# Chunks of x and y at different distances from the weights' buffers, modulo 512 bytes

## The chip, the cores and the metric

One NeuronCore of one Trainium2 chip runs the whole program. The metric is the device time of one launch in microseconds.

## The reference

A linear attention (8 batches, 8 heads, 576 tokens, 64 features), then two MLPs on its output of 4608 tokens by 512 features:

```python
q_s = exp(q - max(q, axis=-1));  q_s /= sum(q_s, axis=-1) + 1e-9
k_s = exp(k - max(k, axis=2));   k_s /= sum(k_s, axis=2) + 1e-9
x = q_s @ (k_s.T @ v)                                # per batch and head, then 4608 x 512
g = x @ w_gate
y = (silu(g) * (x @ w_val)) @ w_out                  # 512 -> 1536 -> 512
h = maximum(maximum(y @ w1, y @ w2), y @ w3)
out = h @ w_out2                                     # 512 -> 768 -> 512
```

q, k and v are float32, the weights are float64, the output is float32.

## The kernel before

The tokens go in 9 blocks of 512. Activations lie with their features on the partitions: x of a block is four chunks (128 features by 512 tokens each), y likewise. A float32 operand of a large product is carried as two float32r parts, hi and lo, and a product as hi*hi + hi*lo + lo*hi (`mm3`, L495). So one 128x512 chunk of a product is three TensorE instructions, each with its own load of 128 columns of weights.

A block is 60 groups in a fixed order. First MLP: for each of 12 slices of 128 hidden features a group G (x by `w_gate`), a group V (x by `w_val`) and a group O (the hidden slice by `w_out`, into four accumulators `acc`). Second MLP: for each of 6 slices W1, W2, W3 (y by a weight slice) and P (the hidden slice by the last weights). Every group is 12 TensorE instructions:

- G, V, W1 to W3 (`proj`): for each of the four chunks c the weights `whi`, `whi`, `wlo` (columns c*128 and on) are loaded, and `xhi`, `xlo`, `xhi` (or `yhi`, `ylo`, `yhi`) of chunk c are streamed, 512 columns each, into one PSUM tile `pm`.
- O (`acc_mm`): `whi`/`wlo` are loaded, `hhi`/`hlo` streamed. P: the other way round, `hhi`/`hlo` loaded and `whi`/`wlo` streamed.

While one product streams, the weights of the next are loaded. Six groups of the first block (`WHOLE`) take plain float32 operands unsplit instead (L525), in two passes each.

`split_hi` (ScalarE, L484) and `split_lo` (VectorE, L489) make `whi` and `wlo` of a group from resident float32 weights or from `plain`, which SyncE loads from a copy in DRAM. Group n's turn issues `split_lo` of n + 3, `split_hi` of n + 4, the products of n, the attention steps of the next block that stand in a table at this group, and the eviction of `pm` (`main_ev`). Both `whi` and `wlo` have five buffers. The attention of the next block makes x with `x_mm` and `x_split` (L388, L389); y is made at the end of O (L578, L579). In the first block, weights are converted from float64 on the way, for which the places of `yhi` and `ylo` serve as staging until y needs them.

The buffers are laid out in the order of their first use, so their places follow from the sizes above them. Modulo 512 bytes within a partition the ones that matter begin here, all buffers of one name alike:

```
raw_g, raw_v, raw_w1..3, kvhi, kvlo, k_sb, q_sb   128
yhi, ylo, qthi                                    224
xhi, xlo, whi, wlo, plain, s, h, hhi, hlo         352
qtlo                                              480
```

A chunk of x or y is 2048 bytes and a weight slice of 128 columns 512 bytes, so all chunks and all slices of a buffer have the same residue. By "distance" the text means the moving operand's start less that of the weights loaded meanwhile, modulo 512: 0 for x against `whi` and `wlo`, 224 - 352 = 384 for y.

Of the kernel before, what the change touches and what calls it, by code (L numbers as in the profile page):

```python
# [8 lines left out]
F32 = mybir.dt.float32  # L9
F32R = mybir.dt.float32r  # L10
# [8 lines left out]
def linear_attention_moe_moe_kernel(  # L19
# [13 lines left out]
):  # L33
    """Per block of 512 tokens: linear attention -> gated MLP -> max-of-three MLP.

    A float32 operand x of the large products is carried as hi + lo, both float32r (12
    significant bits each, so that hi + lo == x), and a product as hi*hi + hi*lo + lo*hi.
    Activations are feature-major (features on partitions) up to the last product.
    """
    nc = tc.nc  # L40
# [17 lines left out]

    ident = sb.tile([128, 128], F32, name="ident")
    raw = {  # L60
# [18 lines left out]
    }  # L79
    # For blocks of 32 by 32 to be transposed: rows are (head of a pair, half of its features,  # L80
    # token of 32), columns (pair, tokens by 32, feature of 32).
    att["qp"] = att["q"].rearrange("p r h d -> p (r h d)").rearrange("p (g n i) -> p g n i", g=HP, i=32)
    # The first block has its tokens in another order (4 p + r in row p of tile r), for long runs
    # in DRAM, and its own staging, where the second MLP's weights will be.
    w = [raw[t].rearrange("p f c n -> p (f c n)") for t in ("W1", "W2", "W3")]
    n, m = R * HH * D, HH * D

    def hrd(a, i):
# [23 lines left out]

    # ---------------------------------------------------------------- attention
    def load_k(t, b, hf):
# [67 lines left out]
    def both(a, tag):  # L182
        """a with the halves of each head's rows (of 32) exchanged."""
        o = sb.tile([128, HP, TB // 32], F32, tag=tag, name=tag)
        for i in range(4):
            p, p1 = 32 * i, 32 * (i ^ 1)
            nc.vector.tensor_copy(out=o[p:p + 32], in_=a[p1:p1 + 32])
        return o
# [163 lines left out]
    def q_t(t, c, g):  # L352
        """Blocks of 32 rows by 32 columns; they already stand where their transposes have to."""
        if g == 0:
            c["qthi"] = sb.tile([128, HP, TB], F32R, tag="qthi", name="qthi")
            c["qtlo"] = sb.tile([128, HP, TB], F32R, tag="qtlo", name="qtlo")
        hi, lo = c["qthi"][:, g, :], c["qtlo"][:, g, :]
        whole = sb.tile([128, TB], F32, tag="o", name="whole", bufs=2)
        nc.vector.transpose(out=whole, in_=t["qp"][:, g].rearrange("p n i -> p (n i)"))
        nc.scalar.copy(out=hi, in_=whole)  # L360
        nc.vector.tensor_tensor(out=lo, in0=whole, in1=hi, op=ALU.subtract)
# [19 lines left out]
    def x_split(px, j, pg):  # L381
        if pg == 0:
            st["x", j] = (
                sb.tile([128, KC, TB], F32R, tag="xhi", name="xhi"),
                sb.tile([128, KC, TB], F32R, tag="xlo", name="xlo"),
            )
        x = st["x", j]
        nc.scalar.copy(out=x[0][:, pg, :], in_=px)  # L388
        nc.vector.tensor_tensor(out=x[1][:, pg, :], in0=px, in1=x[0][:, pg, :], op=ALU.subtract)  # L389

    # ---------------------------------------------------------------- weights
    groups = []
# [26 lines left out]
    def stage_tile(i):  # L419
        """Until the first MLP's output needs their place, four more of them."""  # L420
        if i >= RING or i % 7 < 3:
            return sb.tile([128, 2 * TB], U32, tag="stage", name="stage", bufs=3)
        t, e = divmod(i % 7 - 3, 2)
        return ring[t][:, e, :]

    def load_w(n):
        """The first block takes the weights as they come: pairs of words (low, high) of float64."""
        if n >= len(groups):
            return
        j, kind, f = groups[n]  # L430
        if j == 0:
            staged[n] = stage_tile(done["load"])
            if kind in "OP":
                nc.sync.dma_start(out=staged[n], in_=src[kind][f * 128:(f + 1) * 128, :].bitcast(U32))
            else:
                nc.sync.dma_start(
                    out=staged[n].rearrange("p (c f) -> p c f", c=KC),
                    in_=src[kind][:, f * 128:(f + 1) * 128].bitcast(U32).rearrange("(c p) f -> p c f", p=128),
                )
        elif kind in "OP":  # L440
            plain[n] = sb.tile([128, TB], F32, tag="plain", name="plain", bufs=3)
            nc.sync.dma_start(out=plain[n], in_=kept[kind][f * 128:(f + 1) * 128, :])

    def convert_act(n):
        """float64 words to float32: the high word, scaled as if it were a float32, has its
        exponent field in place for a shift by 3; below float32's range it vanishes. Of the
        low word the upper three bits (0 to 7, the scale keeps it from 8) go to the high word's
        lower half, whose upper half has the sign."""
        j, kind, f = groups[n]
        if kind in "OP":  # L450
            plain[n] = sb.tile([128, TB], F32, tag="plain", name="plain", bufs=3)
        else:
            plain[n] = resident(kind, f)
        words = staged[n].rearrange("p (n t) -> p n t", t=2)
        low, high = words[:, :, 0], words[:, :, 1]
        bits = staged[n].bitcast(U16).rearrange("p (n t) -> p n t", t=4)[:, :, 2]
        nc.scalar.activation(out=plain[n], in_=high.bitcast(F32), func=AF.Abs, scale=2.0 ** -112)  # L457
        nc.scalar.activation(  # L458
            out=bits, in_=low, func=AF.Copy, scale=2.0 ** -29 * (1.0 - 2.0 ** -7), bias=-0.44
        )  # L460
# [17 lines left out]
    def split_hi(n):  # L478
# [3 lines left out]
        hi = sb.tile([128, TB], F32R, tag="whi", name="whi", bufs=5)  # L482
        lo = sb.tile([128, TB], F32R, tag="wlo", name="wlo", bufs=5)
        nc.scalar.copy(out=hi, in_=plain[n])  # L484
        parts[n] = (hi, lo)

    def split_lo(n):
        hi, lo = parts[n]
        nc.vector.tensor_tensor(out=lo, in0=plain.pop(n), in1=hi, op=ALU.subtract)  # L489

    # ---------------------------------------------------------------- main products
    def mm3(o, pairs):
# [6 lines left out]
    def proj(n, act, c0, c1):  # L499
# [3 lines left out]
        if c0 == 0:  # L503
# [3 lines left out]
        mm3(st["p", n], [  # L507
            ((whi[:, cs[c]], wlo[:, cs[c]]), (act[0][:, c, :], act[1][:, c, :]), c == 0, c == KC - 1)
            for c in range(c0, c1)
# [9 lines left out]
    def acc_mm(todo, e0, e1):  # L519
        """The products of O and P: a whole (float32) or as parts."""  # L520
        for e in range(e0, e1):
# [31 lines left out]
    def main_ev(n):  # L553
# [18 lines left out]
        elif kind == "O" and f == F1 - 1:  # L572
            y = (
                sb.tile([128, KC, TB], F32R, tag="yhi", name="yhi"),
                sb.tile([128, KC, TB], F32R, tag="ylo", name="ylo"),
            )
            for e in range(KC):
                nc.scalar.copy(out=y[0][:, e, :], in_=st["acc"][e])  # L578
                nc.vector.tensor_tensor(  # L579
                    out=y[1][:, e, :], in0=st["acc"][e], in1=y[0][:, e, :], op=ALU.subtract  # L580
                )
# [14 lines left out]

    # ---------------------------------------------------------------- schedule
    def attention(j, hf, t):
        """The steps of block j's attention for half of the heads: (slot, step)."""
        c = {}  # L600
# [31 lines left out]
    AHEAD = 3  # L632
    # The first block's conversions: LEAD groups ahead of their use, some of the second MLP earlier.
    order, quota = [], []
# [12 lines left out]
    def loads(upto):  # L647
        """Loads of the first block, in the order of the conversions."""
        while done["load"] < min(upto, GPB):
            load_w(order[done["load"]])  # L650
            done["load"] += 1
# [89 lines left out]

# When the next block's attention goes, by the group that it follows: of the first half of the
# heads and of the second, in the first block and in the others.
SLOTS_FIRST = (
# [26 lines left out]
)  # L771
# Of the first block: conversions whose staging may lie where the first MLP's output will, groups
# whose products take float32 unsplit, conversions ahead, groups that convert one more.
RING = 34
# [6 lines left out]
)  # L781
# What comes before the first group: loads, and steps for a half of the heads, a count of
# conversions or a group ("P": on GpSimd).
LOADS = (
# [45 lines left out]
```

## Time and profile before

| | |
|---|---|
| runs | 1639.6 us median of 3 (1637.58 to 1644.17) |
| profiled execution | span 1635.9 us, 18978 instructions; its own time is not given apart from the span, the median lies 3.7 us above it |
| TensorE busy | 1581.1 us, 97% (6980 products) |
| weight loads busy | 1287.1 us, 79% |
| VectorE, ScalarE busy | 939.7 us, 57%; 741.2 us, 45% |
| granted TensorE clock | 0.995 in the mean |

Busy time of TensorE is the time in which at least one product is in the array; products overlap, so their single durations (some 390 ns) add up to more. How often one starts is read from the start times in the timeline. An instruction is named out<-in; for a product the first input is the moving operand and the second the loaded weights.

### The profile page before, as it was taken

The numbers are of one execution on the slowest core, as the hardware profiler recorded it, in microseconds if no ns is written. First come the engines' busy times: TensorE is split into PE (matmuls) and PEld (weight loads), VectorE is DVE, ScalarE is ACT, GpSimd is POOL, SyncE is SP. The second block draws the span as 40 slices with busy tenths as digits, with TensorE's granted clock in tenths as the row PEclk, the third lists the DMA queues.
The fourth block names the chain that finished last, engine by engine and source line by source line (L and its number), as shares of the span: only waits on it lengthen the run. The fifth ranks groups of instructions, "written<-read, shape, count | busy, mean of one in ns | idle before, by whom it ended". The sixth has DMA issues, their size and how long they took to land.

```text
span 1635.9 us, 18978 instructions
## 1 busy us (share of the span) xinstructions
PE 1581.1 (97%) x6980; PEld 1287.1 (79%) x6980; DVE 939.7 (57%) x1589; ACT 741.2 (45%) x1234; POOL 32.4 (2%) x35
## 2 busy tenths in 40 slices
PE   2699999999999999999999999999999999999999
PEld 1487677888888888888888888888888888888887
DVE  3487785547554765467545754575546644664443
ACT  2799874343434343344334443434343433443332
POOL 1100000000000000000000000000000000000000
PEclk9899999999999999999999999999999999999999
DMA  7484654103310322120411141033102111111100
GB/s 199 119 244 155 190 154 107 33 17 72 79 48 26 68 61 65 33 54 23 111 33 43 38 105 33 16 74 74 52 26 68 52 46 39 26 42 43 33 27 32
DMA packets 197181, 112.93 MB, mean 69 GB/s; under 512 B 145888, under 2 KB 169440, under 8 KB 197088
## 3 DMA queue, kind: packets, MB, share of 16 engines
q1 hardware_dynamic: 197088, 111.72, 25.1%
q8 instruction: 55, 0.90, 0.2%
q14 instruction: 38, 0.31, 0.1%
HBM read 97.52 MB, written 14.16 MB: 68 GB/s over the span
## 4 chain that ended last, share of the span: by engine, by line
PE 89%; ACT 6%; issue 2%; DVE 1%; DMA 1%; POOL 1%; SPq 0%; DVEq 0%; POOLq 0%
PE pm L495 59%; PE acc L495 24%; PE pkv L228 3%; ACT stage L458 2%; ACT whi L484 1%; PE acc L525 1%; PE px L377 1%; PE px L376 1%; PE px L378 1%; ACT raw_w L457 0%; ACT plain L457 0%; DMA raw_w<-in_q_dram 0%; ACT ring_ylo L458 0%; ACT ring_yhi L458 0%; DMA stage<-in_moe_w_dram 0%
## 5 line engine op out<-in xcount | busy, mean ns | idle before, releaser
L495 PE MATMUL pm<-xhi,whi 128*128 128x512 f32 x864 | 339.1, 392 | 3.6 <-ACT s L558 3.6
L495 PE MATMUL pm<-xlo,whi 128*128 128x512 f32 x864 | 336.8, 390 | 0.4 <-DVE xlo L389 0.4
L495 PE MATMUL pm<-xhi,wlo 128*128 128x512 f32 x864 | 336.7, 390 | 0.0
L561 DVE TENSOR_TENSOR h<-s,pm 128x512 f32<-128x512 f32 x108 | 74.3, 688 | 334.8 <-PE pm L495 333.6
L495 PE MATMUL pm<-yhi,whi 128*128 128x512 f32 x648 | 258.3, 399 | 2.3 <-ACT s L565 1.9
L495 PE MATMUL pm<-yhi,wlo 128*128 128x512 f32 x648 | 256.0, 395 | 0.0
L495 PE MATMUL pm<-ylo,whi 128*128 128x512 f32 x648 | 255.7, 395 | 0.2 <-DVE ylo L579 0.2
L515 ACT CAST hhi<-h 128x512 fp32r<-128x512 f32 x156 | 97.5, 625 | 330.7 <-DVE h L561 211.5
L495 PEld LDWEIGHTS pm<-xhi,whi 128*128 128x128 f32 x864 | 162.5, 188 | 39.7 <-ACT s L558 5.0
L495 PEld LDWEIGHTS pm<-xlo,whi 128*128 128x128 f32 x864 | 162.6, 188 | 35.3 <-issue 1.0
L495 PEld LDWEIGHTS pm<-xhi,wlo 128*128 128x128 f32 x864 | 162.5, 188 | 33.6
L495 PE MATMUL acc<-hhi,whi 128*128 128x512 f32 x424 | 164.9, 389 | 0.0
L495 PE MATMUL acc<-hlo,whi 128*128 128x512 f32 x424 | 164.9, 389 | 0.0
L495 PE MATMUL acc<-hhi,wlo 128*128 128x512 f32 x424 | 164.9, 389 | 0.0
L495 PEld LDWEIGHTS pm<-yhi,whi 128*128 128x128 f32 x648 | 121.7, 188 | 34.1 <-ACT s L565 3.2
L558 ACT ACTIVATE s<-pm 128x512 f32<-128x512 f32 x108 | 65.4, 606 | 179.1 <-PE pm L495 179.0
L495 PEld LDWEIGHTS pm<-ylo,whi 128*128 128x128 f32 x648 | 121.7, 188 | 29.2 <-DVE ylo L579 0.5
L495 PEld LDWEIGHTS pm<-yhi,wlo 128*128 128x128 f32 x648 | 121.7, 188 | 29.1
L484 ACT CAST whi<-raw_w 128x512 fp32r<-128x512 f32 x162 | 101.1, 624 | 69.1 <-PE pm L495 55.6
L489 DVE TENSOR_TENSOR wlo<-plain,whi 128x512 fp32r<-128x512 f32 x156 | 106.8, 685 | 17.3 <-ACT whi L484 17.2
L489 DVE TENSOR_TENSOR wlo<-raw_w,whi 128x512 fp32r<-128x512 f32 x162 | 110.0, 683 | 10.2 <-ACT whi L484 10.2
L516 DVE TENSOR_TENSOR hlo<-h,hhi 128x512 fp32r<-128x512 f32 x156 | 108.0, 692 | 12.6 <-ACT hhi L515 0.7
(142 smaller groups left out, 1996.9 us busy)
## 6 DMA issues: line engine op xcount, KB each, us to landing
plain<-kept_o SPq DMA_DIRECT2D x96, 256.0 KB, 2.7
plain<-kept_p SPq DMA_DIRECT2D x48, 256.0 KB, 2.7
out_dram<-o SPq DMA_DIRECT2D x36, 256.0 KB, 2.0
stage<-in_moe_w_dram SPq DMA_DIRECT2D x17, 512.0 KB, 3.8
v_sb<-in_v_dram SPq DMA_DIRECT2D x60, 128.0 KB, 2.7
k_sb<-in_k_dram SPq DMA_DIRECT2D x56, 128.0 KB, 3.2
stage<-in_moe_w_out_dram SPq DMA_DIRECT2D x12, 512.0 KB, 3.7
stage<-in_moe_w_gate_dram SPq DMA_DIRECT2D x6, 512.0 KB, 5.0
```

The source lines that it names most:

```text
L228: nc.tensor.matmul(out=c["pkv"][:, g, :], lhsT=lhsT, rhs=rhs, start=i == 0, stop=i == R)
L376: nc.tensor.matmul(out=px[:, a:e], lhsT=hi, rhs=qhi, start=True, stop=False)
L377: nc.tensor.matmul(out=px[:, a:e], lhsT=hi, rhs=qlo, start=False, stop=False)
L378: nc.tensor.matmul(out=px[:, a:e], lhsT=lo, rhs=qhi, start=False, stop=True)
L458: nc.scalar.activation(out=bits, in_=low, func=AF.Copy, scale=2.0 ** -29 * (1.0 - 2.0 ** -7), bias=-0.44)
L484: nc.scalar.copy(out=hi, in_=plain[n])
L489: nc.vector.tensor_tensor(out=lo, in0=plain.pop(n), in1=hi, op=ALU.subtract)
L495: nc.tensor.matmul(out=o, lhsT=a, rhs=b, start=first and m == 0, stop=last and m == 2)
L515: nc.scalar.copy(out=hi, in_=h)
L516: later.append(lambda: nc.vector.tensor_tensor(out=lo, in0=h, in1=hi, op=ALU.subtract))
L558: nc.scalar.activation(out=st["s"], in_=p, func=AF.Silu)
L561: nc.vector.tensor_tensor(out=h, in0=st["s"], in1=p, op=ALU.mult)
```

## The change

Each of `xhi`, `xlo`, `yhi`, `ylo` becomes a flat tile that is 128 elements (512 bytes) longer, and its four chunks are cut from it at shifts of 0, 8, 48, 80 elements (x) and 0, 32, 48, 96 elements (y): 0, 32, 192, 320 and 0, 128, 192, 384 bytes. To make room, `wlo` has four buffers for five, taken from the pool in `split_lo` and no more in `split_hi`, and `ident` (512 bytes) lies in a part of `raw_w2` that is free until late in the first block. The names `ones` and `diag` are not used. Comments and docstrings are gone, which moves line numbers.

```diff
-    ident = sb.tile([128, 128], F32, name="ident")
...
+    spot = w[1][:, n + (R + 1) * HP * VC:]
+    ident, ones = spot[:, 0:128], spot[:, 128:256]
+    diag = spot[:, 256:512].rearrange("p (g n) -> p g n", g=HP)
...
+    XS, YS = (0, 8, 48, 80), (0, 32, 48, 96)
+
+    def chunks(tag, shifts):
+
+        t = sb.tile([128, KC * TB + 128], F32R, tag=tag, name=tag)
+        return [t[:, e * TB + d:(e + 1) * TB + d] for e, d in enumerate(shifts)]
...
-            st["x", j] = (
-                sb.tile([128, KC, TB], F32R, tag="xhi", name="xhi"),
-                sb.tile([128, KC, TB], F32R, tag="xlo", name="xlo"),
-            )
+            st["x", j] = (chunks("xhi", XS), chunks("xlo", XS))
         x = st["x", j]
-        nc.scalar.copy(out=x[0][:, pg, :], in_=px)
-        nc.vector.tensor_tensor(out=x[1][:, pg, :], in0=px, in1=x[0][:, pg, :], op=ALU.subtract)
+        nc.scalar.copy(out=x[0][pg], in_=px)
+        nc.vector.tensor_tensor(out=x[1][pg], in0=px, in1=x[0][pg], op=ALU.subtract)
...
         hi = sb.tile([128, TB], F32R, tag="whi", name="whi", bufs=5)
-        lo = sb.tile([128, TB], F32R, tag="wlo", name="wlo", bufs=5)
         nc.scalar.copy(out=hi, in_=plain[n])
-        parts[n] = (hi, lo)
+        parts[n] = (hi, None)
 
     def split_lo(n):
-        hi, lo = parts[n]
+        hi = parts[n][0]
+        lo = sb.tile([128, TB], F32R, tag="wlo", name="wlo", bufs=4)
+        parts[n] = (hi, lo)
         nc.vector.tensor_tensor(out=lo, in0=plain.pop(n), in1=hi, op=ALU.subtract)
...
-            ((whi[:, cs[c]], wlo[:, cs[c]]), (act[0][:, c, :], act[1][:, c, :]), c == 0, c == KC - 1)
+            ((whi[:, cs[c]], wlo[:, cs[c]]), (act[0][c], act[1][c]), c == 0, c == KC - 1)
...
-            y = (
-                sb.tile([128, KC, TB], F32R, tag="yhi", name="yhi"),
-                sb.tile([128, KC, TB], F32R, tag="ylo", name="ylo"),
-            )
+            y = (chunks("yhi", YS), chunks("ylo", YS))
             for e in range(KC):
-                nc.scalar.copy(out=y[0][:, e, :], in_=st["acc"][e])
+                nc.scalar.copy(out=y[0][e], in_=st["acc"][e])
                 nc.vector.tensor_tensor(
-                    out=y[1][:, e, :], in0=st["acc"][e], in1=y[0][:, e, :], op=ALU.subtract
+                    out=y[1][e], in0=st["acc"][e], in1=y[0][e], op=ALU.subtract
                 )
```

The buffers begin at the same residues as before: y at 224, x, `whi` and `wlo` at 352. So the distances are 0, 32, 192 and 320 for x's chunks 0 to 3, and 384, 0, 64 and 256 for y's: seven different values, 0 among both.

The instructions and their order on every engine stay as they were, but for the names. What changes is a wait: 186 of the subtractions into `wlo` now wait for TensorE, which has to be done with the buffer's last use. On VectorE, around the groups of the first MLP in the second block, the rows read before:

```order
L561 TENSOR_TENSOR h<-s,pm 128x512 [waits PE_49,Activation_49]
L489 TENSOR_TENSOR wlo<-raw_g,whi 128x512 [waits Activation_49]
L516 TENSOR_TENSOR hlo<-h,hhi 128x512 [waits Activation_49]
L489 TENSOR_TENSOR wlo<-raw_v,whi 128x512 [waits Activation_49]
L561 TENSOR_TENSOR h<-s,pm 128x512 [waits PE_49,Activation_49]
```

With the change, at the same place:

```order
L568 TENSOR_TENSOR h<-s,pm 128x512 [waits PE_49,Activation_49]
L496 TENSOR_TENSOR wlo<-raw_g,whi 128x512 [waits Activation_49]
L523 TENSOR_TENSOR hlo<-h,hhi 128x512 [waits Activation_49]
L496 TENSOR_TENSOR wlo<-raw_v,whi 128x512 [waits PE_49,Activation_49]
L568 TENSOR_TENSOR h<-s,pm 128x512 [waits PE_49,Activation_49]
```

One of the two subtractions into `wlo` waits for TensorE as well (PE_49); nothing has moved.

## Rows read from the trace of the kernel before

**Rows 1.** The page: span, busy time by engine, granted clock in 40 slices.

```profile
span 1635.9 us, 18978 instructions
...
PE 1581.1 (97%) x6980; PEld 1287.1 (79%) x6980; DVE 939.7 (57%) x1589; ACT 741.2 (45%) x1234; POOL 32.4 (2%) x35
...
PEclk9899999999999999999999999999999999999999
```

**Rows 2.** The page: the chain of waits that ended last, by line.

```profile
PE pm L495 59%; PE acc L495 24%; PE pkv L228 3%; ACT stage L458 2%; ACT whi L484 1%; PE acc L525 1%; PE px L377 1%; PE px L376 1%; PE px L378 1%; ACT raw_w L457 0%; ACT plain L457 0%; DMA raw_w<-in_q_dram 0%; ACT ring_ylo L458 0%; ACT ring_yhi L458 0%; DMA stage<-in_moe_w_dram 0%
```

**Rows 3.** Groups of instructions: count, busy us, mean ns of one, idle before.

```profile
L495 PE MATMUL pm<-xhi,whi 128*128 128x512 f32 x864 | 339.1, 392 | 3.6 <-ACT s L558 3.6
...
L495 PE MATMUL pm<-yhi,whi 128*128 128x512 f32 x648 | 258.3, 399 | 2.3 <-ACT s L565 1.9
L495 PE MATMUL pm<-ylo,whi 128*128 128x512 f32 x648 | 255.7, 395 | 0.2 <-DVE ylo L579 0.2
...
L495 PE MATMUL acc<-hhi,whi 128*128 128x512 f32 x424 | 164.9, 389 | 0.0
...
L495 PE MATMUL acc<-whi,hhi 128*128 128x512 f32 x200 | 78.2, 391 | 0.0
```

**Rows 4.** Timeline of PE, products with x: start us, us; twelve from first to last.

```profile
259.90 0.39 PE L495 MATMUL pm<-xhi,whi 128*128 128x512 f32 x1
...
262.62 0.39 PE L495 MATMUL pm<-xhi,whi 128*128 128x512 f32 x1
```

**Rows 5.** Timeline of PE, products with y, 24 up to `pkv`.

```profile
399.66 0.40 PE L495 MATMUL pm<-yhi,whi 128*128 128x512 f32 x1
399.90 0.39 PE L495 MATMUL pm<-ylo,whi 128*128 128x512 f32 x1
400.12 0.40 PE L495 MATMUL pm<-yhi,wlo 128*128 128x512 f32 x1
...
405.26 1.05 PE L228 MATMUL pkv<-v_sb,k_sb 128*128 128x130 f32 x8
```

**Rows 6.** Timeline of PE, a group P behind y, up to the next y.

```profile
372.84 0.40 PE L495 MATMUL acc<-whi,hhi 128*128 128x512 f32 x1
373.08 0.40 PE L495 MATMUL acc<-wlo,hhi 128*128 128x512 f32 x1
373.31 0.40 PE L495 MATMUL acc<-whi,hlo 128*128 128x512 f32 x1
373.55 0.39 PE L495 MATMUL acc<-whi,hhi 128*128 128x512 f32 x1
...
374.93 0.39 PE L495 MATMUL acc<-whi,hhi 128*128 128x512 f32 x1
...
375.61 0.40 PE L495 MATMUL pm<-yhi,whi 128*128 128x512 f32 x1
```

**Rows 7.** Timeline of PE, around `px` in two blocks.

```profile
425.60 0.40 PE L495 MATMUL acc<-whi,hlo 128*128 128x512 f32 x1
425.83 0.28 PE L376 MATMUL px<-qthi,kvhi 128*128 128x256 f32 x1
...
1422.58 0.39 PE L495 MATMUL pm<-yhi,wlo 128*128 128x512 f32 x1
1422.81 0.39 PE L376 MATMUL px<-qthi,kvhi 128*128 128x512 f32 x1
1423.05 0.40 PE L377 MATMUL px<-qtlo,kvhi 128*128 128x512 f32 x1
1423.28 0.39 PE L378 MATMUL px<-qthi,kvlo 128*128 128x512 f32 x1
1423.52 0.39 PE L495 MATMUL pm<-yhi,whi 128*128 128x512 f32 x1
```

**Rows 8.** Plain float32 products: eight passes in the timeline, and their group.

```profile
205.64 3.59 PE L525 MATMUL acc<-plain,h 128*128 128x512 f32 x8
...
L525 PE MATMUL acc<-plain,h 128*128 128x512 f32 x32 | 14.6, 598 | 0.0
```

**Rows 9.** Timeline of DVE in the second block.

```profile
302.06 0.69 DVE L489 TENSOR_TENSOR wlo<-raw_v,whi 128x512 fp32r<-128x512 f32 x1 [0.46 <-ACT whi L484]
307.09 0.69 DVE L561 TENSOR_TENSOR h<-s,pm 128x512 f32<-128x512 f32 x1 [4.34 <-PE pm L495]
```

**Rows 10.** Busy us (and instructions) of PE, PEld, DVE, ACT, POOL in a stretch of the first block.

```profile
100.00:300.00 200.00, 193.81 (x816) 150.30 (x816) 150.01 (x266) 149.21 (x212) 3.72 (x3) 0.99 0.52 155
```

More of the change, by code (lines that the diff above doesn't have):

```diff
@@ L482, in split_hi, with split_lo @@
         hi = sb.tile([128, TB], F32R, tag="whi", name="whi", bufs=5)
-        lo = sb.tile([128, TB], F32R, tag="wlo", name="wlo", bufs=5)
         nc.scalar.copy(out=hi, in_=plain[n])
+        parts[n] = (hi, None)
+    def split_lo(n):
+        hi = parts[n][0]
+        lo = sb.tile([128, TB], F32R, tag="wlo", name="wlo", bufs=4)
         parts[n] = (hi, lo)
-    def split_lo(n):
-        hi, lo = parts[n]
         nc.vector.tensor_tensor(out=lo, in0=plain.pop(n), in1=hi, op=ALU.subtract)
```

## The prediction

> **What bounds the kernel.** The page first: TensorE (PE) is busy for 97% of the span, VectorE (DVE) for 57%, ScalarE (ACT) for 45%, and the granted clock reads 9 in every slice but one, which is the 2.4 GHz level [rows 1]. The chain of waits says the same: products of `pm` at L495 make up 59% of the span and those of `acc` 24% [rows 2]. So the time is the number of TensorE instructions times their spacing, and a change pays only if it moves that spacing or makes TensorE wait.
>
> The spacing comes from the timeline, as the difference of two start times (a duration of 0.39 includes the drain, which overlaps the next product). With x as the moving operand, twelve products take 262.62 - 259.90 = 2.72 us, 226.7 ns each [rows 4]. With y, 24 products take 405.26 - 399.66 = 5.60 us, 233.3 ns each, in a pattern of a longer and a shorter one [rows 5]. Both are 128x512 with the same number type at the same clock. The groups of instructions agree: 390 to 392 ns of one with x, 395 to 399 with y, 389 with `hhi` [rows 3]. What differs is the address: x, `whi` and `wlo` begin at 352 modulo 512, y at 224. While a product streams x or y, the weights of the next product are loaded from `whi` or `wlo`, so the distance of moving operand and load is 0 for x and 384 for y. Distance does matter here, by 6.6 ns per product between these two.
>
> One more group matters. The products of P stream `whi` while `hhi` or `hlo` is loaded, at distance 0 as well, but directly behind y. There the first four begin 0.24, 0.23 and 0.24 us apart, and all twelve take 375.61 - 372.84 = 2.77 us, 230.8 ns each, although the last three are back at 0.227 [rows 6]. So 226.7 is a state that distance 0 settles into after some products; what ran before decides how soon. In O, behind x, it is there throughout (389 ns of one), in P not quite (391) [rows 3].
>
> **The change, part by part.** (1) *x leaves distance 0.* There are 3 x 864 = 2592 products with x [rows 3], 648 per chunk. Chunk 0 stays at 0; chunks 1, 2 and 3 go to 32, 192 and 320, 1944 products in all. No row has these distances. The lower bound is a product with nothing in its way: the eight passes of plain float32 products run at half rate and take 3.59 us with the 0.60 of the last [rows 8], so (3.59 - 0.60)/7 = 0.427 per pass and 213.6 at full rate. The upper bound is the other distances that the trace has at 512 columns: `px` and the y product ahead of it run at 96, 352 and 384, and those four take 1423.52 - 1422.58 = 0.94 us, 235 each, and single ones read 0.24; a product at 224 takes 425.83 - 425.60 = 0.23 us [rows 7]. Everything in the trace that is not settled lies between 230.8 and 235, on both sides of y's 233.3. I take 232 for an unknown distance, midway between P behind y and y, since those two have the most products behind them. 1944 x (232 - 226.7) = **+10.3 us**.
>
> (2) *x's chunk 0 and the O products lose their settled state.* In a G group chunk 0 follows a settled O; in a V group it follows chunk 3 of G, so half of its 648 products start unsettled: 324 x (230.8 - 226.7) = **+1.3 us**. The 3 x 424 products of O [rows 3] now stand behind x's chunk 3 as P's stand behind y; P reads 391 against O's 389, so 1272 x 2 ns = **+2.5 us**. Lower bound of both: nothing, if the new distances settle too.
>
> (3) *y.* Of 3 x 648 = 1944 products [rows 3], 486 per chunk, chunk 0 stays at 384. Chunk 1 comes to 0, three products at a time between others, so as P's unsettled ones: 486 x (230.8 - 233.3) = -1.2 us. Chunks 2 and 3 go to 64 and 256, both unknown: 972 x (232 - 233.3) = -1.3 us. Together **-2.5 us**. P stays behind y's chunk 3 as before.
>
> (4) *Four `wlo` buffers for five.* 186 subtractions on VectorE now wait for the products of the group that has just gone by. Queued behind such a subtraction are the subtraction of `hlo` and the next eviction of `pm`. A group is 2.72 us, and the `wlo` written then is used three groups, 8.2 us, later; one subtraction takes 0.69, and VectorE sits idle for 4.3 us in front of the eviction of `h` [rows 9]. So the wait is taken from idle time: 0. Without that cover, in the first block, VectorE is busy 150 of 200 us and TensorE already loses 6 [rows 10]; I allow 0 to +3 us there.
>
> (5) *`ident` in a piece of `raw_w2`, and every buffer moved by a multiple of 32 bytes:* the transposes of the first block read it before that place is converted; no term.
>
> Sum: 10.3 + 1.3 + 2.5 - 2.5 = **+11.6 us** on the profiled execution's span of 1635.9. The median of the runs, 1639.6, lies 3.7 above it, and nothing outside the span changes, so I forecast 1639.6 + 11.6 = **1651 us**, 0.7% slower.
>
> **The rule of two ports.** The row first: the same product is spaced 226.7 ns behind x and 233.3 behind y [rows 4, 5]. The Trainium skill, "SBUF — State Buffer", section "Who interferes with whom", gives TensorE two independent read ports, one for the moving operand and one for weight loads, and says that "PE and ACT never wait on anyone". By that rule no distance would matter and the sum would be 0; the two rows speak against it.
>
> The fp32 passes come within a nanosecond of one column per cycle at half rate [rows 8]. The Trainium skill, "TensorE: Matmul & The Clock Gate", section "Back-to-back issue gap", puts a lone 512-column product at N/2.4 + 2.5, an estimate of 215.8 ns; by it all five new distances could gain 11 to 18 ns a product, and the sum would be near -36 us. No fp32r row of this trace runs there.
>
> **The rivals.** With p for the mean spacing at the five unknown distances the sum is 1944(p - 226.7) + 972(p - 233.3) + 2600 ns. It is 0 at p = 228.0, and 0.5% of the time (8.2 us, about what a measurement can tell from no change) away at 225.2 and 230.8.
>
> *Free distances, faster.* If the load and the moving read pass each other unhindered at some distances, p falls below 225.2. With two of x's three new chunks and one of y's two at 213.6 and the others at 232: 1296 x -13.1 + 648 x 5.3 + 486 x -19.7 + 486 x -1.3 + 2600 ns = -21 us, **1618 us**. For it: distance matters, and most residues have no row. Against: the rows at distances 0, 96, 224, 352 and 384 show nothing steadily under 226.7 [rows 4 to 7]. Chance 0.23.
>
> *Near balance.* The new distances settle like 0 does, or mix, p between 225.2 and 230.8: 226.7 everywhere gives -6.4 us plus the 2.6 of term 2 and chunk 1, **about 1636**. Chance 0.22.
>
> *Distance does nothing*, and y is slower for another reason (what the evictions beside it do, say): **1640**. For it only the rule above. Chance 0.08.
>
> *The `wlo` wait decides*, in the first block where its cover is thin: it has an effect from the point where VectorE comes to a subtraction less than 0.7 us before its product; then +3 us on top of any case, **1654** with mine. Chance 0.04, inside slower.
>
> *Mine*, p above 230.8: 0.47 with the last.
>
> **How the numbers follow.** Slower by over 0.5% 0.47, within 0.5% 0.22 + 0.08 = 0.30, faster 0.23. From the bounds: p = 222 gives 1624, p = 236 gives 1663, and with a tenth of the chance beyond either end the range is 1624 to 1663. The likeliest case's own range, p from 231 to 236, is 1648 to 1663.
>
> **What would show it.** In the timeline of the changed kernel each chunk's three products have their own spacing: 226 to 231 for x's chunk 0, 230 to 236 for the others, and O no longer at 227 throughout. In the groups of instructions x's mean rises from 390 to about 395 while y's stays at 394 to 398. The `wlo` rows wait for `pm` or `acc`, and `h` and `s` don't move against TensorE. Wrong if any chunk runs near 214, if x stays at 390 in all chunks, or if TensorE shows new idle time for `wlo`.

## The result and the profile after

The changed kernel takes 1651.35 us in the median of 4 runs (1647.88 to 1652.49) against 1639.74 for the kernel before, a ratio of 1.0068 with a 95% interval of 1.0049 to 1.0088: 11 us slower, between 8 and 14. The forecast was 1651 us.

The page of the changed kernel has the same shares as before to within one per cent [rows 1]. TensorE is busy for 1596.0 us, where it was 1581.1, at a granted clock of 0.997 (0.995 before). VectorE is busy for 10 us more too, but so it is in e1 below (949.0 us), which is faster than the kernel before. The 134 instructions more are semaphore instructions of VectorE, for its new waits:

```profile
span 1650.7 us, 19112 instructions
...
PE 1596.0 (97%) x6980; PEld 1291.8 (78%) x6980; DVE 949.7 (58%) x1589; ACT 741.3 (45%) x1234; POOL 31.2 (2%) x35
...
PE pm L502 58%; PE acc L502 24%; PE pkv L237 3%; ACT stage L464 2%; ACT whi L489 1%; PE acc L532 1%; ACT raw_w L463 1%; PE px L386 1%; PE px L385 1%; PE px L387 0%; ACT plain L463 0%; ACT ring_ylo L464 0%; ACT ring_yhi L464 0%; DMA stage<-in_moe_w_out_dram 0%; DMA stage<-in_moe_w_dram 0%
```

The groups of instructions show where [rows 3]: products with x went from 390 to 392 ns of one to 395 and 396, O's from 389 to 392 in two of its three kinds, y's are within 1 ns of where they were:

```profile
L502 PE MATMUL pm<-xhi,whi 128*128 128x512 f32 x864 | 342.5, 396 | 3.2 <-ACT s L565 3.2
L502 PE MATMUL pm<-xlo,whi 128*128 128x512 f32 x864 | 341.5, 395 | 0.3 <-DVE xlo L395 0.3
...
L502 PE MATMUL pm<-yhi,whi 128*128 128x512 f32 x648 | 258.9, 399 | 1.9 <-ACT s L572 1.6
...
L502 PE MATMUL pm<-ylo,whi 128*128 128x512 f32 x648 | 255.3, 394 | 0.2 <-DVE ylo L583 0.2
...
L502 PE MATMUL acc<-hlo,whi 128*128 128x512 f32 x424 | 166.3, 392 | 0.0
L502 PE MATMUL acc<-hhi,whi 128*128 128x512 f32 x424 | 166.1, 392 | 0.0
L502 PE MATMUL acc<-hhi,wlo 128*128 128x512 f32 x424 | 165.1, 389 | 0.0
```

The timeline of TensorE shows both losses in one place, the end of a V group, the O behind it and the next G:

```profile
277.04 0.39 PE L502 MATMUL pm<-xhi,whi 128*128 128x512 f32 x1
277.27 0.40 PE L502 MATMUL pm<-xlo,whi 128*128 128x512 f32 x1
...
278.43 0.39 PE L502 MATMUL acc<-hhi,whi 128*128 128x512 f32 x1
278.66 0.40 PE L502 MATMUL acc<-hlo,whi 128*128 128x512 f32 x1
...
279.59 0.39 PE L502 MATMUL acc<-hhi,wlo 128*128 128x512 f32 x1
279.81 0.39 PE L502 MATMUL acc<-hhi,whi 128*128 128x512 f32 x1
...
281.17 0.39 PE L502 MATMUL pm<-xhi,whi 128*128 128x512 f32 x1
281.40 0.39 PE L502 MATMUL pm<-xlo,whi 128*128 128x512 f32 x1
281.62 0.39 PE L502 MATMUL pm<-xhi,wlo 128*128 128x512 f32 x1
281.85 0.40 PE L502 MATMUL pm<-xhi,whi 128*128 128x512 f32 x1
282.09 0.39 PE L502 MATMUL pm<-xlo,whi 128*128 128x512 f32 x1
```

The six products of x's chunks 2 and 3 take 278.43 - 277.04 = 1.39 us, 232 ns each, where twelve at distance 0 took 227 each [rows 4]. O starts unsettled: its first five come 0.232 apart (279.59 - 278.43 = 1.16 us), and from 279.81 to 281.17 six take 1.36, 227 each. Chunk 0 of the next G, behind a settled O, keeps that; with chunk 1 the spacing is up again (282.09 - 281.85 = 0.24).

Below, a spacing is the mean difference of neighbouring start times, with differences above 262 ns left out, since there TensorE waits. By chunk it reads, in ns:

| | chunk 0 | chunk 1 | chunk 2 | chunk 3 | all |
|---|---|---|---|---|---|
| x, distance | 0: 229.4 | 32: 233.7 | 192: 231.0 | 320: 229.9 | 231.0 (before 226.8) |
| y, distance | 384: 231.4 | 0: 232.0 | 64: 233.1 | 256: 232.7 | 232.3 (before 233.0) |
| y before, distance | 384: 233.5 | 384: 232.2 | 384: 234.2 | 384: 232.0 | 233.0 |

O rose from 226.7 to 228.6, P from 228.7 to 228.8.

### The profile page after: what moved, and what is told of

Same layout as the page of the kernel before. It is cut to its first block, busy times and chain, and to the rows that moved or that the text cites. A ratio compares the mean times of both kernels' runs of the same rounds, so it can differ in the third digit from the quotient of the medians.

```text
span 1650.7 us, 19112 instructions
## 1 busy us (share of the span) xinstructions
PE 1596.0 (97%) x6980; PEld 1291.8 (78%) x6980; DVE 949.7 (58%) x1589; ACT 741.3 (45%) x1234; POOL 31.2 (2%) x35
## 4 chain that ended last, share of the span: by engine, by line
PE 88%; ACT 7%; issue 3%; DVE 1%; DMA 1%; POOL 1%; POOLq 0%; DVEq 0%
PE pm L502 58%; PE acc L502 24%; PE pkv L237 3%; ACT stage L464 2%; ACT whi L489 1%; PE acc L532 1%; ACT raw_w L463 1%; PE px L386 1%; PE px L385 1%; PE px L387 0%; ACT plain L463 0%; ACT ring_ylo L464 0%; ACT ring_yhi L464 0%; DMA stage<-in_moe_w_out_dram 0%; DMA stage<-in_moe_w_dram 0%
## 5 line engine op out<-in xcount | busy, mean ns | idle before, releaser
L502 PE MATMUL pm<-xlo,whi 128*128 128x512 f32 x864 | 341.5, 395 | 0.3 <-DVE xlo L395 0.3
L502 PE MATMUL pm<-xhi,wlo 128*128 128x512 f32 x864 | 341.3, 395 | 0.0
L496 DVE TENSOR_TENSOR wlo<-raw_v,whi 128x512 fp32r<-128x512 f32 x108 | 75.2, 697 | 128.7 <-PE pm L502 128.7
```

The costliest lines, as they stand in the source:

```text
L502: nc.tensor.matmul(out=o, lhsT=a, rhs=b, start=first and m == 0, stop=last and m == 2)
```

## The experiments

All are the changed kernel with other values of `XS` and `YS`, unless more is shown, so all have its buffers. The medians of the kernel before in the three sets of runs were 1638.2, 1639.0 and 1639.3 us. Times without a ratio are of one run.

**Everything at 0, everything at 384, the buffers alone, one other pair.** Does the distance do it, and does each distance have its own level or does only the change within a group cost?

```diff
-    XS, YS = (0, 8, 48, 80), (0, 32, 48, 96)
+    XS, YS = (0, 0, 0, 0), (32, 32, 32, 32)      # e1: x and y at 0
+    XS, YS = (96, 96, 96, 96), (0, 0, 0, 0)      # e2: x and y at 384
+    XS, YS = (0, 0, 0, 0), (0, 0, 0, 0)          # e3: x at 0, y at 384, as before
+    XS, YS = (80, 80, 80, 80), (48, 48, 48, 48)  # e4: x at 320, y at 64
```

> All chunks of x and y at distance 0 (x shifted by 0, y by 128 bytes), the rest as in the changed kernel. Theory (the spacing follows the distance, and 0 settles at 226.7 ns): y falls from 233.0 to 226.7 ns as x did before, 1944 products x -6.3 = -12 us against the kernel before, and P no longer stands behind an unsettled y, 600 x -2 = -1 us: 1639.7 - 13 = 1627 us. Rival (y is slower for what runs beside it, not for its place): y stays at 233, 1640 us.

> All chunks of x and y at distance 384 (x shifted by 384 bytes, y by 0). Theory: x rises from 226.8 to y's 233.0 ns, 2592 x 6.2 = +16 us, and O behind it by 2 ns, 1272 x 2 = +2.5 us: 1658 us. Rival (distance does nothing, the buffers or the shift itself cost time): x stays at 227, 1640 us.

> Four buffers for wlo, ident inside raw_w2 and the longer tiles as in the changed kernel, but all shifts 0: the distances of the kernel before (0 for x, 384 for y). Theory: the wait for the buffer is hidden, 1639.7 us within 3 us, x at 226.8 and y at 233.0 ns. Rival (the wait of wlo costs what the change costs): 1651 us with the spacings of the kernel before.

> All chunks of x at 320 and all of y at 64. In the changed kernel the three products of x's chunk at 320 took 229.9 ns in the mean, those of y's chunk at 64 took 233.1. Theory (each distance has its own level): x 229.9, 2592 x 3.1 = +8 us, O +2.5 us, y unchanged: 1650 us. Rival (any distance settles at 226.7 if it is the same for all chunks, and what costs time is the change of distance within a group): x and y at 226.7, 1627 us.

e1: 1628.5 us, ratio 0.9929 (0.9916 to 0.9941); y fell to 227.0 ns, P to 227.5. Its groups of instructions now read alike for x and y, the first of each three carrying the waits:

```profile
span 1626.7 us, 19112 instructions
...
L502 PE MATMUL pm<-xlo,whi 128*128 128x512 f32 x864 | 337.1, 390 | 0.4 <-DVE xlo L395 0.4
...
L502 PE MATMUL pm<-yhi,whi 128*128 128x512 f32 x648 | 254.9, 393 | 2.5 <-ACT s L572 1.9
...
L502 PE MATMUL pm<-ylo,whi 128*128 128x512 f32 x648 | 252.3, 389 | 0.2 <-DVE ylo L583 0.2
```

e2: 1655.1 us, ratio 1.0094 (1.0080 to 1.0108); x rose to 233.0 ns, O to 227.8, so O lost 1.1 ns where 2 were expected. Its groups with x, against 390 to 392 ns of one before:

```profile
L502 PE MATMUL pm<-xhi,whi 128*128 128x512 f32 x864 | 342.8, 397 | 3.0 <-ACT s L565 3.0
...
L502 PE MATMUL pm<-xlo,whi 128*128 128x512 f32 x864 | 340.9, 395 | 0.3 <-DVE xlo L395 0.3
```

With e1 and e2 the same products run at either level by their place alone, and what runs beside x or y is no cause.

e3: 1639.2 us, ratio 0.9998 (0.9989 to 1.0007), spacings as before. Its waits on VectorE are there, and cost nothing; they have taken the place of the wait in front of `h`, which was 333.6 us in the kernel before:

```profile
DVE h L568 <- PE pm L502: 173.4, 95, 2.4
DVE wlo L496 <- PE pm L502: 167.9, 106, 2.4
...
DVE wlo L496 <- PE acc L502: 51.3, 81, 0.7
```

e4: 1644.1 us, ratio 1.0035 (1.0025 to 1.0045). x at 320 runs at 229.5 ns and y at 64 at 229.5. The rival, that any uniform distance settles at 226.7, falls: each distance has its level. But the level is also that of what stands around it: y's chunk at 64 took 233.1 among other distances, 229.5 among its own. O behind x lost 3.8 ns, more than behind any other, and took back part of what y gained.

**The same distances in other places, and more distances.**

```diff
-    XS, YS = (0, 8, 48, 80), (0, 32, 48, 96)
+    XS, YS = (0, 0, 0, 0), (48, 48, 48, 48)        # f1: x and y at 0, with the lines below
+    XS, YS = (64, 64, 64, 64), (64, 64, 64, 64)    # f2: x at 256, y at 128
+    XS, YS = (48, 48, 48, 48), (40, 40, 40, 40)    # f3: x at 192, y at 32
+    XS, YS = (112, 112, 112, 112), (72, 72, 72, 72)  # f4: x at 448, y at 160
...
         if pg == 0:
+            if j == 0:
+                sb.tile([128, 16], F32, tag="pad", name="pad")
             st["x", j] = (chunks("xhi", XS), chunks("xlo", XS))
```

> As e1, but 64 bytes are laid in front of xhi, so that x, whi, wlo, hhi and hlo begin at 416 modulo 512 instead of 352, and y is shifted by 192 bytes to begin there too. All distances are 0 as in e1. Theory (the distance between the moving operand and the load counts): x and y at 226.7 ns and 1628 us as e1. Rival (the place itself counts, 352 being a good one): other spacings for x, O and y, above 228 ns, and a time near or above 1640 us.

> All chunks of x at 256, all of y at 128. If only 0 settles: both between 229 and 234 ns, x +2 to +7 ns on 2592 products, O +2 to +4 on 1272, y -4 to +1 on 1944, so 1640 to 1660 us. Rival (there are distances under 226.7): one of them below 225, under 1630 us.

> All chunks of x at 192, all of y at 32. In the changed kernel x's chunk at 192 took 231.0 ns in the mean and the one at 32 took 233.7. If only 0 settles: both between 229 and 234 ns, 1640 to 1660 us. Rival (there are distances under 226.7): one of them below 225, under 1630 us.

> All chunks of x at 448, all of y at 160. If only 0 settles: both between 229 and 234 ns, 1640 to 1660 us. Rival (there are distances under 226.7): one of them below 225, under 1630 us.

f1: 1628.4 us, ratio 0.9945 (0.9926 to 0.9965), x at 226.8 and y at 227.2 ns. So it is the distance that counts and not the place, as far as a move by 64 bytes can show.

f2: 1638.8 us in one run, and this was not expected by either side: x at 256 runs at 226.8 ns as at 0, y at 128 at 233.0 as at 384. The period is 256 bytes, not 512. f3 and f4 say the same with x at 192 and at 448, both at 233.3 ns and both at 1656 to 1659 us. Here x has settled at another level: 2475 of its 2592 gaps between starts are 233 or 234 ns in f3, and 2457 in f4.

```profile
L502 PE MATMUL pm<-xhi,whi 128*128 128x512 f32 x864 | 339.0, 392 | 3.6 <-ACT s L565 3.6
L502 PE MATMUL pm<-xlo,whi 128*128 128x512 f32 x864 | 337.0, 390 | 0.4 <-DVE xlo L395 0.4
...
L502 PE MATMUL pm<-ylo,whi 128*128 128x512 f32 x648 | 255.8, 395 | 0.2 <-DVE ylo L583 0.2
```

These are f2's groups; for x and y they are those of the kernel before [rows 3]. f3's, in the next fence, have x at 394 and more:

```profile
L502 PE MATMUL pm<-xhi,whi 128*128 128x512 f32 x864 | 342.3, 396 | 2.8 <-ACT s L565 2.8
L502 PE MATMUL pm<-xlo,whi 128*128 128x512 f32 x864 | 340.6, 394 | 0.3 <-DVE xlo L395 0.3
```

**The last multiples of 32, a half step, the period in one group, and a shorter load.**

```diff
-    XS, YS = (0, 8, 48, 80), (0, 32, 48, 96)
+    XS, YS = (56, 56, 56, 56), (56, 56, 56, 56)    # g1: x at 224, y at 96
+    XS, YS = (4, 4, 4, 4), (28, 28, 28, 28)        # g2: x at 16, y at 496
+    XS, YS = (0, 0, 64, 128), (32, 32, 96, 96)     # g3: 0, 0, 256, 512 and 0, 0, 256, 256
+    XS, YS = (0, 0, 0, 0), (32, 32, 32, 32)        # g4: as e1, with the lines below
...
-        mm3(st["p", n], [
-            ((whi[:, cs[c]], wlo[:, cs[c]]), (act[0][c], act[1][c]), c == 0, c == KC - 1)
-            for c in range(c0, c1)
-        ])
+        for c in range(c0, c1):
+            p, (hi, lo) = st["p", n], (act[0][c], act[1][c])
+            half = slice(c * 128, c * 128 + 64)
+            nc.tensor.matmul(out=p, lhsT=whi[:, cs[c]], rhs=hi, start=c == 0, stop=False)
+            nc.tensor.matmul(out=p[0:64], lhsT=wlo[:, half], rhs=hi, start=False, stop=False)
+            nc.tensor.matmul(out=p, lhsT=whi[:, cs[c]], rhs=lo, start=False, stop=c == KC - 1)
```

> All chunks of x at 224, all of y at 96. The earlier runs gave x at 256 the spacing of x at 0 (226.8 ns), x at 448 that of x at 192 (233.3) and y at 128 that of y at 384 (233.0). If the distance counts modulo 256, 96 and 224 are the last multiples of 32 without a uniform run. Theory: both lie between 229 and 235 ns like the others, 1640 to 1665 us. Rival: one of them is under 226.7 ns, and the time under 1640 us.

> All chunks of x at 16, all of y at 496 (240 modulo 256), half a step of 32 bytes to either side of 0. If places count in steps of 32 bytes or more, each reads as one of its neighbours: x as 0 (226.8 ns) or 32 (233), y as 0 or 224. If they count in finer steps, other values; under 226.7 ns would be a better place than 0. Time 1628 to 1660 us.

> x's chunks at 0, 0, 256 and 512, y's at 0, 0, 256 and 256. Theory (the distance counts modulo 256 and 0 settles): x and y at 226.7 to 227.0 ns in every chunk, 1628 us as e1. Rival (512 is the period, or any change of distance within a group unsettles): chunks at 256 above 229 ns, O above 228, 1640 us or more.

> As e1 (all distances 0), but the products of G, V and W1 to W3 come as hi*hi, lo*hi, hi*lo, and the one with wlo loads only 64 of its 128 columns, so half of that part is left out of the result. The load that runs beside the first product of each chunk is half as long. Theory (the load's reads take time from the moving operand's): that product's spacing falls from 226.7 towards the 213.6 ns of an undisturbed one, to about 220; the other two stay at 226.7 or above. Rival (the 13 ns above 213.6 are a fixed cost of each product): all three stay at 226.7.

g3: 1628.6 us, ratio 0.9937 (0.9921 to 0.9954), x 226.8 and y 227.0 ns, every chunk within 226.7 to 227.3. A change of distance by 256 or 512 within a group unsettles nothing:

```profile
L502 PE MATMUL pm<-xlo,whi 128*128 128x512 f32 x864 | 337.2, 390 | 0.4 <-DVE xlo L395 0.4
...
L502 PE MATMUL pm<-ylo,whi 128*128 128x512 f32 x648 | 252.3, 389 | 0.0
```

g1: 1660.9 us, x 233.4 and y 233.6. g2: 1652.0 us, x 231.6 and y 233.9: 16 bytes off is not 0 any more, nor its neighbour at 32.

g4: 1645.6 us, slower than e1, and both sides of it fall. The load is shorter, but no kind of product got closer to 213.6:

```profile
L517 PEld LDWEIGHTS pm<-xhi,whi 128*128 128x128 f32 x864 | 163.1, 189 | 43.1 <-ACT s L567 5.5 <-issue 1.0 <-PE acc L534 0.2
...
L518 PEld LDWEIGHTS pm<-xhi,wlo 128*64 128x64 f32 x864 | 116.6, 135 | 37.1 <-issue 0.8 <-DVE wlo L496 0.5
...
L517 PE MATMUL pm<-xhi,whi 128*128 128x512 f32 x864 | 341.2, 395 | 4.4 <-ACT s L567 4.4
L518 PE MATMUL pm<-xhi,wlo 128*64 128x512 f32 x864 | 340.2, 394 | 0.0
L519 PE MATMUL pm<-xlo,whi 128*128 128x512 f32 x864 | 339.0, 392 | 0.1
```

The half load takes 135 ns for 189, and the product beside it is spaced 229.1 in the mean, 2.3 more than with the whole load in e1; the other two at 230.3 and 229.3. At distance 0 the state of 226.7 is lost in this run, and the 13 ns above 213.6 did not shrink. But the edit changes two things, the length of one load in three and the order of the three products. No run has that order with whole loads, so which of the two loses the state isn't shown, and what the 13 ns are is open.

All uniform distances together, modulo 256 (x gives 0, 16, 192 and 224, y gives 32, 96, 128, 160 and 240, both give 64; x at 384 in e2 reads 233.0 as y does):

| distance modulo 256 | 0 | 16 | 32 | 64 | 96 | 128 | 160 | 192 | 224 | 240 |
|---|---|---|---|---|---|---|---|---|---|---|
| spacing, ns | 226.8 | 231.6 | 233.3 | 229.5 | 233.6 | 233.0 | 234.1 | 233.3 | 233.4 | 233.9 |

A second measure needs no choice of which gaps to count: the time from the 1001st start of a product to the last (6980 in every trace). Before that point the traces differ by up to 6 us, also where the places are alike (270.3 us before, 271.9 in f2), and most of it lies in the first 200 products: 73.7 us in the kernel before, 78.5 in the changed one, 73.7 to 78.7 in the experiments.

| before, e3, f2 | e1, g3 | f1 | g4 | e4 | after | g2 | e2 | f3 | f4 | g1 |
|---|---|---|---|---|---|---|---|---|---|---|
| 1336.711 | 1325.584 | 1325.744 | 1340.641 | 1341.537 | 1346.987 | 1350.326 | 1351.786 | 1353.738 | 1354.758 | 1354.756 |

The three kernels of the first column agree to the nanosecond over 1.3 ms, though y stands at 384 in two and at 128 in the third, x at 0 and at 256, and `wlo` has five buffers in one and four in the others; so do e1 and g3. f1 is 0.16 us off e1, with the same distances for x and y but others for the `px` products.

## Why the prediction was right

*Term 1, x leaves distance 0.* The three new distances average 231.5 ns, 232 was taken: 1944 x (231.5 - 226.8) = +9.1 us for +10.3. The single ones lie from 229.9, just under the 230 to 236 that the prediction gave, to 233.7. The lower bound of 213.6 was never approached, the upper one of 235 not either.

*Term 2, settled states lost.* Chunk 0 rose to 229.4, 648 x 2.6 = +1.7 us for +1.3. It did so in the way that was forecast: behind O it reads 226.7 as before, behind chunk 3 of a group with x 231.7, where 230.8 was taken. O rose by 1.9, 1272 x 1.9 = +2.4 us for +2.5. That O suffers for a change of x, with no operand of its own moved, was the less plain part of the sum, and P behind y [rows 6] had shown it.

*Term 3, y.* 1944 x (232.3 - 233.0) = -1.4 us for -2.5, and most of it not where it was expected. Chunk 1 came to distance 0 and gained 0.3 ns on its own 232.2, not 2.5: alone at 0 between others it did not settle. Chunk 2 gained 1.2 and chunk 3 lost 0.7. Chunk 0, which kept its distance of 384 and for which nothing was taken, gained 2.1 ns, 486 x 2.1 = 1.0 us; that this comes from its new neighbours is likely and not shown. Here the working took 0 and 256 for two distances, one known and one unknown; by f2 and g3 they are one, as are x's 320 and y's 64, so of the seven values five differ. The sum did not depend on it, since 232 stood for any unknown one and chunk 3 read 232.7.

*Terms 4 and 5, `wlo` and `ident`,* were 0 and are 0 by e3, to the nanosecond after the first thousand products. The first thousand took e3 0.7 us longer than the kernel before, within what they vary.

The measured terms add up to 9.1 + 1.7 + 2.4 - 1.4 = +11.8 us over all products, as if none were hidden. The trace has +10.3 from the 1001st product on (x +9.3, O +2.1, y -1.2). Products 201 to 1000 take as long as before, 196.6 us: the spacings add 1.2 us there, and waits of TensorE in the first block give it back. The first 200 take 4.8 us longer, 3.5 of it in differences above 262 ns, so in waits, and only 0.3 in the spacing of the 104 products with x among them; that stretch varies from run to run (e3, with the old distances, has 1.5 of these 4.8).

The medians differ by 11.6. The mechanism and the size of the large terms were right, but that the forecast fits to within 1 us is partly luck: term 1 was 1.2 us too high and term 3 1.1 too low, and the steady loss that the trace shows is 10.3.

*The rivals and the range.* The lower end of the range was reckoned wrongly: with p = 222 the prediction's own sum gives 1639.6 - 17.5 = 1622, not 1624. "Free distances" falls: ten places modulo 256, none under 226.7. "Near balance" put p between 225.2 and 230.8; p came out at 232.0, from x's three new chunks and y's at 64 and 256, weighted by their products. "Distance does nothing" falls by e1 and e2. The rule of the Trainium skill behind it ("SBUF — State Buffer", "Who interferes with whom") does not hold here in the sense that the prediction drew from it, that no distance would matter: by their distance alone the same product is spaced 226.8 or 233.0.

## What to carry to other kernels

Where TensorE is the bound and every product comes with its own load (here float32r products of 512 columns with loads of 128, the only kind tried), look at the spacing of starts by moving operand: if two groups of one shape differ by a few ns, compare where the moving buffers and the weights' buffers begin, modulo 256 bytes. Put them all at the same residue, with one distance for all products that follow each other; here that is e1, 1628.5 us, 0.7% under the kernel before and 1.4% under the changed one. A probe that spreads the places to see which is good measures the unsettling too, so give each place a run of its own.

## What was not expected

The period of 256 bytes, and that distance 0 is not free of a price but a state: behind another distance it takes some products at 224 to 236 ns before 226.7 is reached, nine in [rows 6]. Of the 98 stretches of O products in a trace, 75 take five in the changed kernel and 95 take ten in e4, and some P groups of the kernel before take ten as well. g4, with its half loads in another order, loses it. In every trace the starts in stretches of six or more products at 226 or 227 ns, taken modulo 6.667 ns, agree: within 0.2 ns over 47 stretches in the kernel before, within 0.7 ns in the worst of the others, once a steady drift of 2.2 to 2.5 ns over the run is taken off, though unsettled products and waits lie between the stretches. Modulo 13.333 ns they don't agree. 226.67 is 34 times 6.667, and the level of 233.3 that x settles at with distance 192 is 35 times. So, as these figures read, a beat of 6.667 ns that runs on by itself goes into the spacing beside the distance; which part of the chip has it, and why the distance counts modulo 256 bytes, these runs don't tell.
